# An attention and two expert layers in one program: the first tile's transposes of x moved into the drain of attention

## The chip, the cores and the metric

The program runs on one core of a Trainium2 chip. The metric is device time in microseconds of that core, from one launch to its end. Three runs of the kernel before gave 890.12, 890.15 and 888.39 us; their median is 890.12 us. Of one execution there is a profile.

## The reference, cut to what matters

Three layers follow each other: an attention with a window of 128 keys and 4 sink keys (batch 4, 8 heads, 768 positions, 64 per head), a first layer of 8 experts in which each token goes to its best expert, and a second one in which tokens are given to experts by rank up to a capacity of 384.

```
x = attention(q, k, v)                        # [3072, 512] after the heads are joined
logits = x @ w_gate + modality_bias[modality_id]
e_idx  = argmax(logits, axis=1)
gate_w = softmax(logits)[e_idx]
for e in range(8):                            # first layer of experts
    h = relu(x[e_idx == e] @ w1[e])           # 512 -> 1024
    out[e_idx == e] = gate_w * (h @ w2[e])    # 1024 -> 512
logits2 = out @ w_gate2                       # second layer: capacity 384 for each expert
out2[assigned == e] = relu(out[...] @ w21[e]) @ w22[e]
```

## The kernel before, in words

The program is written as one order of instructions for all engines; each engine takes its own in that order and waits on semaphores.

**Attention** goes over 48 groups (`NG`): a group is two blocks of 128 queries of a pair of heads. An iteration k of the loop at the end of `attention` works on several groups at once. It does the scores of group k, the transposes of the probabilities of group k-1 (`trans`, `tcopy`), the sink transposes of group k-3 (`sinktr` on TensorE, `sinkout` on ScalarE, which writes `skT`), the products with v of group k-2 (`pv`, which fills the PSUM tile `po`), and for group k-4 the copy of `po` to `oT` (ScalarE, L403), the product that makes rows of x of it (`rows`: L411 from `skT`, then L413 from `oT`, both into the PSUM tile `px`) and the division by the softmax sums (`xout`, VectorE, `rv`, `xb`, `lp`). `px` has one buffer, so `rows` of a group waits for `lp` of the group before. After the last group four more iterations run without scores: the **drain**.

**The gate** of a batch (`after_batch`) is cut into pieces `v1` to `v4` and six scatters, which a list of work in the background (`BG`) hands out: `bg.pop` takes the next piece at fixed places of the main loop. A piece that stands with a number in front waits until a model of TensorE's time has gone on by so much since the last piece. The piece `v3b` has two matmuls with the one-hot `oh` (L590, L591).

**The first expert layer** (`moe1`, which calls `Ffn.run`) goes over six tiles of 512 tokens, which are gathered from x by expert. Each tile has 8 steps; a step s does 12 matmuls of the first product into `ph` (L940) and 12 of the second into `y0` to `y3` (L883). Both operands are split into a part of full precision for the matmul and a residue: `xh`, `xl` of the tokens, `w1h`, `w1l` and `w2h`, `w2l` of the weights, `hh`, `hl` of the hidden layer. ScalarE writes the first of each, VectorE the second as the difference. `xprep` turns one of the four 128-column parts of the gathered tokens `xg` with four transposes on TensorE (L750), copies to `xh` (L751) and takes the residue `xl` (L752). The tiles 0 and 1 take tokens of the first two batches alone, so that their gathers can be issued during attention.

Before step 0, `Ffn.run` prepares the first tile: the weights of chunk 0, the four parts of x, then eight matmuls that write nothing of use (`warm`, L759), then chunk 1:

```
if i == ahead:
    src.idle()
    poll_w(1)
    for d in range(4):
        prep(js[0], d, ("tr", "ph", "y1", "y2")[d])
    if pre:
        self.warm(WARM1)
```

All tiles of this layer lie in memory that attention's tiles had, so their first writers wait for attention's last readers.

Of the kernel before, what the change touches and what calls it, by code (L numbers as in the profile page):

```python
# [21 lines left out]
NP = H // 2  # L22
# [160 lines left out]

def attention(ctx, tc, g, qT, kT, v4, vsT, vsR, wg, put_x, after_batch, bg, drain=True):
    nc = tc.nc
# [46 lines left out]
    nc.sync.dma_start(wgp, wgv)  # L232
    vst = wk.tile([128, B * NP, 96], F32, name="vst", bufs=1)
    nc.sync.dma_start(vst, vsT)
    vsx = wk.tile([96, B * NP, 72], F32, name="vsx", bufs=1)
    nc.sync.dma_start(vsx[:, :, 0:64], vsR)
# [206 lines left out]
    for k in range(NG + LRO):  # L443
# [47 lines left out]
class Gate:  # L491
# [60 lines left out]
    def after_batch(self, b, lp):  # L552
# [16 lines left out]
        def v1b():  # L569
            nc.vector.tensor_reduce(mx, lg, axis=AX.X, op=OP.max)  # L570
            nc.vector.tensor_tensor(dl, lg, bc(mx[:, :, None], [128, NB, E]), op=OP.subtract)

        def v2():
            nc.scalar.activation(ex, dl, AF.Exp)
# [159 lines left out]
class Ffn:  # L734
    def __init__(self, ctx, tc, g, tag, tpe=384, rawpool=None, vsplit=False):
        self.tc, self.nc, self.g = tc, tc.nc, g
        self.wk = ctx.enter_context(tc.tile_pool(name=tag, bufs=2))
        self.ps = ctx.enter_context(tc.tile_pool(name=tag + "p", bufs=1, space=PSUM))
        self.trbufs, self.tpe, self.vsplit = 1, tpe, vsplit
        self.rawpool = rawpool or self.wk  # L740
        self.xt = {}

    def xprep(self, j, A, xg, d, tag="tr"):
        nc, w = self.nc, 128 * A
        if d == 0:
            self.xt[j] = (self.wk.tile([128, 4, self.tpe], F32R, name="xh"), self.wk.tile([128, 4, self.tpe], F32R, name="xl"))
# [14 lines left out]
    def run(self, js, w1, w2, src, yout, hook=None, xp=((6, 0), (6, 2), (7, 0), (7, 2)), LEAD=3, LAG=2, pre=None, onx=None, more=(), mark=lambda s, n: None):  # L761
# [77 lines left out]
        def split1(c, part):  # L839
# [5 lines left out]
            if part == 0:  # L845
                ch[0][c] = (wk.tile([128, 512], F32R, name="w1h", bufs=LEAD + 2),
                            wk.tile([128, 512], F32R, name="w1l", bufs=LEAD + 2))
            h, lo = [t if small(c) else t.rearrange("p (d f) -> p d f", d=4) for t in ch[0][c]]
# [325 lines left out]
class Direct:  # L1174
# [6 lines left out]
    def load(self, i, c):  # L1181

        f, e = self.f, self.src.ereg(self.j)
        for m in (2 * c, 2 * c + 1):
            t = f.wk.tile([128, 512], F32R, name=("w1", "w2")[i] + "hl"[m % 2], bufs=4).bitcast(F32)
# [76 lines left out]

def moe1(tc, g, G, src, rt, w1, w2, wg2, wg2T):
    nc = tc.nc
    with ExitStack() as ctx:
# [52 lines left out]
        def mark(s, n):  # L1318
# [3 lines left out]
            for i in {(6, 1): (0,), (8, 1): (1,)}.get((f5, n), ()):  # L1322
# [3 lines left out]
        hook = lambda: bg.pop(2 if len(bg.q) > 12 or bg.q and isinstance(bg.q[0], tuple) else 1)  # L1326
        raw, xgs = f.run(big, w1, w2, src, yout, hook=hook, pre=(src.raw, dict(src.xg)), onx=onx, LEAD=2,
                         more=[t.j for t in small], mark=mark)
# [722 lines left out]
def tile_kernel(ctx, tc, qT, kT, v4, vsT, vsR, mid, wg, mbias, w1, w2, wg2, wg2T, w21, w22, cst, out):  # L2051
# [9 lines left out]
    with ExitStack() as c1:  # L2061
# [53 lines left out]
```

## Time and profile before

| | before |
|---|---|
| median of three runs | 890.12 us |
| runs | 888.39 to 890.15 us |
| the profiled execution's own time | 890.04 us |
| its span, first to last instruction | 888.3 us |
| TensorE busy | 841.3 us, 95% of the span |
| VectorE, ScalarE, GpSimd busy | 608.2, 386.8, 356.3 us |
| last attention matmul starts | 206.78 us |
| first matmul of the expert layer starts | 211.41 us |

A busy TensorE is not at its peak: its matmul ends are modelled, and the granted clock (PEclk on the page) tells at which of its two speeds it ran. An idle engine costs something only where another waits for it, so the table's shares say little of a change at one place; for that the timeline of the stretch from 200 to 225 us is read.

### The profile page before, as it was taken

The page shows a single profiled execution, that of the slowest core. Times are in us where ns is not written, and L with a number is a line of the kernel's source. Part 1 is how long each engine was busy: PE and PEld are TensorE (multiplying, and loading weights), DVE is VectorE, ACT ScalarE, POOL GpSimd, SP SyncE. Part 2 cuts the span into 40 slices and gives each one's busy share as a digit, 9 for nine tenths or more (in the row PEclk, how much of TensorE's full clock was granted, in tenths as well). Part 3 has the DMA queues.
Part 4 walks back from the last instruction along what each step waited for, and adds up shares of the span by engine and source line. Part 5 has one row for each costly group of instructions (what it writes and reads, how often), then busy time and mean ns, then how long its engine had stood idle before and what let it go on. Part 6 is the DMA issues. An engine that isn't in the chain of part 4 may idle for free.

```text
span 888.3 us, 15299 instructions
## 1 busy us (share of the span) xinstructions
PE 841.3 (95%) x5051; PEld 666.4 (75%) x5051; DVE 608.2 (68%) x1769; ACT 386.8 (44%) x1093; POOL 356.3 (40%) x555
## 2 busy tenths in 40 slices
PE   8889898898999999999999987999999999999997
PEld 4556666566888888888888645778788878789996
DVE  3868787876759697978886458768777776663320
ACT  3677676774334343434342214233333333445431
POOL 2776655574430202010000006535464737376561
PEclk9999999999999999999999989999999999999999
DMA  8344473549364444444346324323444424346301
GB/s 250 106 142 145 111 178 93 153 120 339 96 138 148 143 142 143 142 143 142 106 144 220 127 77 158 123 103 131 143 146 159 164 95 152 117 155 207 101 37 39
DMA packets 69774, 123.90 MB, mean 139 GB/s; under 512 B 9652, under 2 KB 22454, under 8 KB 69559
## 3 DMA queue, kind: packets, MB, share of 16 engines
q1 hardware_dynamic: 62998, 103.41, 37.1%
q0 software_dynamic: 6688, 19.43, 6.9%
q8 instruction: 42, 0.69, 0.4%
q14 instruction: 46, 0.37, 0.2%
HBM read 103.11 MB, written 19.71 MB: 138 GB/s over the span
## 4 chain that ended last, share of the span: by engine, by line
PE 74%; DVE 10%; issue 5%; ACT 4%; POOL 3%; DMA 3%; SPq 0%; POOLq 0%; DVEq 0%; ACTq 0%
PE ph L940 27%; PE y L883 26%; PE sp L306 4%; PE po L378 2%; ACT P L335 2%; PE tr L750 2%; PE rt L1569 2%; PE pt L343 2%; DMA xg<-xs,idx 1%; PE rc L1428 1%; PE px L413 1%; DVE mx L325 1%; DVE sc L150 1%; DMA vst<-in_vsT_dram 1%; DVE cmp L150 1%
## 5 line engine op out<-in xcount | busy, mean ns | idle before, releaser
L950 ACT ACTIVATE hh<-ph 128x384 fp32r<-128x384 f32 (+1 forms) x112 | 60.1, 537 | 273.7 <-PE ph L940 265.1
L940 PE MATMUL ph<-xh,w1h 128*128 128x384 f32 (+1 forms) x448 | 170.0, 380 | 0.0
L940 PE MATMUL ph<-xh,w1l 128*128 128x384 f32 (+1 forms) x448 | 162.6, 363 | 0.0
L940 PE MATMUL ph<-xl,w1h 128*128 128x384 f32 (+1 forms) x448 | 161.9, 364 | 0.0
L883 PE MATMUL y<-w2h,hh 128*128 128x512 f32 x384 | 155.5, 405 | 0.0
L883 PE MATMUL y<-w2h,hl 128*128 128x512 f32 x384 | 151.3, 394 | 0.0
L883 PE MATMUL y<-w2l,hh 128*128 128x512 f32 x384 | 151.2, 394 | 0.0
L951 DVE SCALAR_TENSOR_TENSOR hl<-ph,hh 128x384 fp32r<-128x384 f32 (+1 forms) x112 | 68.5, 611 | 107.9 <-ACT hh L950 102.1
L836 POOL TENSOR_TENSOR w2l<-w2r,w2h 128x512 fp32r<-128x512 f32 x64 | 88.7, 1393 | 64.8 <-ACT w2h L832 33.9
L1106 POOL DMA_INDIRECT xg<-xd,ent x26 | 29.1, 1120 | 189.5 <-DMA ent<-idtab 100.5
L1130 DVE SCALAR_TENSOR_TENSOR junk<-yr,wgb 128x512 f32<-128x512 f32 x160 | 103.1, 685 | 0.0
L940 PEld LDWEIGHTS ph<-xh,w1h 128*128 128x128 f32 x448 | 86.0, 192 | 10.2
L335 ACT ACTIVATE P<-sp,mx 128x132 f32<-128x132 f32 x192 | 69.0, 367 | 55.6 <-DVE mx L325 30.0
L940 PEld LDWEIGHTS ph<-xh,w1l 128*128 128x128 f32 x448 | 85.7, 191 | 9.6
L940 PEld LDWEIGHTS ph<-xl,w1h 128*128 128x128 f32 x448 | 85.0, 190 | 7.8
L883 PEld LDWEIGHTS y<-w2h,hl 128*128 128x128 f32 x384 | 72.5, 189 | 16.0
L883 PEld LDWEIGHTS y<-w2h,hh 128*128 128x128 f32 x384 | 73.1, 190 | 11.4
L883 PEld LDWEIGHTS y<-w2l,hh 128*128 128x128 f32 x384 | 72.9, 190 | 11.4
L306 PE MATMUL sp<-kr,qs 64*128 64x260 f32 (+1 forms) x384 | 60.0, 411 | 17.1 <-ACT P L335 17.0
L850 ACT ACTIVATE w1h<-w1r 128x512 fp32r<-128x512 f32 x112 | 69.7, 624 | 5.7 <-DMA w1r<-in_w_dram 3.3
L832 ACT ACTIVATE w2h<-w2r 128x512 fp32r<-128x512 f32 x112 | 69.6, 624 | 0.4 <-DMA w2r<-in_w_dram 0.4
L855 DVE TENSOR_TENSOR w1l<-w1r,w1h 128x512 fp32r<-128x512 f32 x80 | 65.5, 819 | 3.5 <-ACT w1h L850 3.5
(362 smaller groups left out, 1414.5 us busy)
## 6 DMA issues: line engine op xcount, KB each, us to landing
w1r<-in_w_dram SPq DMA_DIRECT2D x30, 1024.0 KB, 6.5
w2r<-in_w_dram SPq DMA_DIRECT2D x30, 1024.0 KB, 7.4
kr<-in_kT_dram SPq DMA_DIRECT2D x16, 396.0 KB, 3.7
qr<-in_qT_dram SPq DMA_DIRECT2D x16, 384.0 KB
vr<-in_v_dram SPq DMA_DIRECT2D x16, 384.0 KB, 4.9
xd<-xb SPq DMA_DIRECT2D x16, 384.0 KB
xs<-yr SPq DMA_DIRECT2D x24, 256.0 KB, 5.9
wgb<-in_wg2T_dram SPq DMA_DIRECT2D x1, 2048.0 KB
```

Of the source, the lines that this page charges most:

```text
L306: nc.tensor.matmul(sp[:, hd, c0:260], qs[o:o + 64, 128 * i:128 * i + 128], kr[o:o + 64, k0:k0 + 260 - c0], start=True, stop=True)
L335: nc.scalar.activation(z.P[:, n % 2, hd, :], s.sp[:, hd, 128:260], AF.Exp, bias=s.mx[:, hd:hd + 1], accum_out=z.sm[:, n % 2, hd:hd + 1])
L832: nc.scalar.activation(ch[1][c][0], r[:, q, :], AF.Copy)
L836: eng.tensor_tensor(lo, r[:, q, :], h.bitcast(F32), op=OP.subtract)
L850: nc.scalar.activation(h, v, AF.Copy)
L855: eng.tensor_tensor(lo, v, h.bitcast(F32), op=OP.subtract)
L883: nc.tensor.matmul(o, l, r, start=(first and i == 0), stop=(end and i == 2))
L940: nc.tensor.matmul(ph, wp[:, c, :], xp_[:, c, 0:NTK], start=(d == 0 and i == 0), stop=(d == 3 and i == len(cut[d]) - 1))
L950: nc.scalar.activation(hh, ph, AF.Relu)
L951: nc.vector.scalar_tensor_tensor(hl, ph, 0.0, hh.bitcast(F32), op0=OP.max, op1=OP.subtract)
L1106: self.nc.gpsimd.indirect_dma_start(out=self.xg[j][:, a, :], out_offset=None, in_=self.G.xd[0:k, :], in_offset=bass.IndirectOffsetOnAxis(a ...
L1130: nc.vector.scalar_tensor_tensor(junk, yr[:, 0:DM], 1.0, wgb[:, e, :], op0=OP.mult, op1=OP.mult, accum_out=lg[:, e:e + 1])
```

## The change

Three things are done. First, a class `Ahead` holds tiles in memory of their own: `xh0` and `xl0` for the tokens of every second tile, and two pairs of weight tiles. At the end of each of the four drain iterations, `Ahead.step` does one of the four parts of the first tile's preparation: four transposes into a PSUM tile of attention's `sp`, the copy to `xh`, the residue `xl`. In the last two of them it also splits a chunk of the first weights. Second, `Ffn.run` takes these as done: no preparation and no warm-up matmuls stand before step 0. Third, the gate pieces of the last batch each carry the number 1.4 (`SP`), so that they are spaced by the model of TensorE's time; its four empty pieces are dropped, and the exponential of that batch is a piece of its own.

```diff
+        if not live:
+            fa.step(k - NG, lambda: ps.tile([128, 2, 512], F32, name="sp", bufs=2)[:, 0])
         bg.pop(1)
-    if drain:
-        bg.drain()
...
+    def step(self, n, bank):
+        nc, src = self.nc, self.src
+        if n == 0:
+            self.x = self.xpair()
+        xh, xl = self.x
+        p, xg = bank(), src.xg[0]
+        for a in range(TPE // 128):
+            nc.tensor.transpose(p[:, 128 * a:128 * a + 128], xg[:, a, 128 * n:128 * n + 128], self.g.ident)
+        nc.scalar.activation(xh[:, n, :], p, AF.Copy)
+        nc.vector.tensor_tensor(xl[:, n, :], p, xh[:, n, :].bitcast(F32), op=OP.subtract)
+        if n in (2, 3):
+            c = n - 2
+            r = src.raw[0][0][:, :, 128 * c:128 * c + 128]
+            h, lo = self.w1[c] = self.tile("w1h", c), self.tile("w1l", c)
+            v = [t.rearrange("p (d f) -> p d f", d=4) for t in (h, lo)]
+            nc.scalar.activation(v[0], r, AF.Copy)
+            nc.vector.tensor_tensor(v[1], r, v[0].bitcast(F32), op=OP.subtract)
...
-        v = [v1, v1b, v2, v2b, v3] + [nop] * (4 if b == B - 1 else 1) + [v3b, v3c, v4]
+        v = [v1, v1b, lambda: (vx(), v2()), v2b, v3, nop, v3b, v3c, v4]
...
-            self.bg.add(*v, *[lambda f=f, h=h: (f(), h()) for f, h in zip(la, sc6)], lambda: self.done.add("x"))
+            last = [v1, v1b, vx, v2, v2b, v3, v3b, v3c, v4] + [lambda f=f, h=h: (f(), h()) for f, h in zip(la, sc6)]
+            self.bg.add(*[(SP, f) for f in last], lambda: self.done.add("x"))
...
-        ahead = 1 if pre else AHEAD
+        if pre:
+            steps = []
+            poll_w(1)
+            self.fa, self.xt[js[0]], done[0] = pre[2], pre[2].x, 2
+            for c in range(2):
+                ch[0][c] = pre[2].w1[c]
+                for n in ("w1h", "w1l"):
+                    self.ring[n] = c
...
-                if pre:
-                    self.warm(WARM1)
```

The first tiles of attention that hold the sink keys (`vst`, `vsx`) now lie in the same memory as `xh0` and `xl0`; they are read only in the first iterations.

On ScalarE the drain's instructions stood like this before (`skT` and `oT` are attention's, the `xh` rows and `w1h` belong to the expert layer):

```order
L348 ACTIVATE t_3112<-pt_3107 128x512
L397 ACTIVATE skT_3114<-sp_3105 96x128
L403 ACTIVATE oT_3157<-po_3091 128x256
L397 ACTIVATE skT_3161<-sp_3159 96x128
L403 ACTIVATE oT_3184<-po_3142 128x256
L397 ACTIVATE skT_3188<-sp_3186 96x128
L403 ACTIVATE oT_3202<-po_3169 128x256
L850 ACTIVATE w1h_3250<-w1r_3128 128x512
L751 ACTIVATE xh_3254<-tr_3256 128x512
```

After the last `oT` came the expert layer's own work. In the changed kernel the same stretch of ScalarE's queue reads:

```order
L348 ACTIVATE t_3115<-pt_3110 128x512
L397 ACTIVATE skT_3117<-sp_3108 96x128
L510 ACTIVATE xh0_3160<-sp_3162 128x512
L403 ACTIVATE oT_3169<-po_3094 128x256
L397 ACTIVATE skT_3173<-sp_3171 96x128
L510 ACTIVATE xh0_3160<-sp_3194 128x512
L403 ACTIVATE oT_3203<-po_3145 128x256
L397 ACTIVATE skT_3207<-sp_3205 96x128
L510 ACTIVATE xh0_3160<-sp_3218 128x512
L517 ACTIVATE w1h0_3225<-w1r_3131 128x512
L403 ACTIVATE oT_3232<-po_3181 128x256
L510 ACTIVATE xh0_3160<-sp_3261 128x512
```

Each of the last three `oT` now has a copy to `xh` ahead of it, the last one a `w1h` too. On TensorE the same drain, from the second of its iterations to the expert layer, stood like this before (`xg` is the first tile's gathered tokens, `px` the rows of x):

```order
L392 MATMUL sp_3159<-cst_62,psk2_174 96x128
L411 MATMUL px_3163<-bd_169,skT_3114 128x288
L413 MATMUL px_3163<-rw_165,oT_3157 128x144 x2
L378 MATMUL po_3142<-lu_3094,vr_2755 64x128 x2
...
L413 MATMUL px_3190<-rw_165,oT_3184 128x144 x2
L411 MATMUL px_3205<-bd_169,skT_3188 128x288
L413 MATMUL px_3205<-rw_165,oT_3202 128x144 x2
L750 MATMUL tr_3256<-cst_62,xg_2793 128x128 x4
```

Behind these rows came the other twelve transposes, the eight warm-up matmuls and step 0. In the changed kernel TensorE has:

```order
L509 MATMUL sp_3162<-cst_62,xg_2796 128x128 x4
L392 MATMUL sp_3171<-cst_62,psk2_177 96x128
L411 MATMUL px_3175<-bd_172,skT_3117 128x288
L413 MATMUL px_3175<-rw_168,oT_3169 128x144 x2
...
L509 MATMUL sp_3218<-cst_62,xg_2796 128x128 x4
L411 MATMUL px_3235<-bd_172,skT_3207 128x288
L413 MATMUL px_3235<-rw_168,oT_3232 128x144 x2
L509 MATMUL sp_3261<-cst_62,xg_2796 128x128 x4
L993 MATMUL ph_3291<-xh0_3160,w1h0_3225 128x512
```

Four transposes stand ahead of each remaining `rows`, the last four behind the last one, and step 0 (L993, the old L940) follows at once. Its first matmul waits for the residue `xl0` of the last part, since that is read from a bank that `ph` takes over. The two matmuls of the last batch's gate piece `v3b` move on TensorE from step 4, between its two products, to behind the first transposes of the next tile in step 6; those of the batch before stay where they were, behind the 12 matmuls of step 1.

## Rows read from the trace of the kernel before

**Rows 1.** The page's busy time of TensorE: us, share, instructions.

```profile
PE 841.3 (95%) x5051; PEld 666.4 (75%) x5051; DVE 608.2 (68%) x1769; ACT 386.8 (44%) x1093; POOL 356.3 (40%) x555
```

**Rows 2.** Timeline of TensorE, drain to step 1: start, us, line, idle and releaser.

```profile
202.82 0.31 PE L392 MATMUL sp<-cst,psk 128*96 128x128 f32 x1
...
203.10 0.65 PE L413 MATMUL px<-rw,oT 128*128 128x144 f32 x4
203.69 1.31 PE L378 MATMUL po<-lu,vr 128*64 128x128 f32 x16
204.93 0.32 PE L392 MATMUL sp<-cst,psk 128*96 128x128 f32 x1
...
206.57 0.37 PE L411 MATMUL px<-bd,skT 96*128 96x288 f32 x1 [0.71 <-DVE rv L425]
206.78 0.66 PE L413 MATMUL px<-rw,oT 128*128 128x144 f32 x4
208.09 0.63 PE L750 MATMUL tr<-cst,xg 128*128 128x128 f32 x4 [0.66 <-PE px L413]
...
209.87 1.89 PE L759 MATMUL y<-wz 128*128 128x512 bf16 x8
211.41 0.58 PE L940 MATMUL ph<-xh,w1h 128*128 128x512 f32 x1
...
214.36 0.39 PE L940 MATMUL ph<-xh,w1h 128*128 128x512 f32 x1
```

**Rows 3.** Timeline of ScalarE, drain and step 0.

```profile
202.34 0.38 ACT L403 ACTIVATE oT<-po 128x256 f32<-128x256 f32 x1 [0.32 <-PE po L378]
...
208.23 0.63 ACT L850 ACTIVATE w1h<-w1r 128x512 fp32r<-128x512 f32 x1 [2.35 <-DVE lp L431]
...
214.56 0.60 ACT L950 ACTIVATE hh<-ph 128x512 fp32r<-128x512 f32 x1 [2.71 <-PE ph L940]
```

**Rows 4.** Timeline of all engines, a part of x prepared for the second tile.

```profile
248.14 0.60 ACT L751 ACTIVATE xh<-tr 128x512 fp32r<-128x512 f32 x1
248.63 0.62 ACT L832 ACTIVATE w2h<-w2r 128x512 fp32r<-128x512 f32 x1
...
251.41 0.60 PE L750 MATMUL tr<-cst,xg 128*128 128x128 f32 x4
...
252.04 0.60 ACT L751 ACTIVATE xh<-tr 128x512 fp32r<-128x512 f32 x1 [2.78 <-PE tr L750]
...
252.67 0.69 DVE L752 TENSOR_TENSOR xl<-tr,xh 128x512 fp32r<-128x512 f32 x1 [1.13 <-ACT xh L751]
```

**Rows 5.** Timeline of TensorE, gate matmuls between steps 1 and 2, second product.

```profile
219.95 0.18 PE L590 MATMUL rt<-oh,tri 128*128 128x48 bf16 x1 [2.71 <-DVE oh L581]
...
224.41 0.39 PE L883 MATMUL y<-w2h,hh 128*128 128x512 f32 x1
```

**Rows 6.** Windows of TensorE: stretch, its us, PE busy, granted clock, DMA, GB/s.

```profile
142.00:145.40 3.40, 1.63 (x13) 1.00 0.58 220
145.40:148.80 3.40, 3.40 (x20) 0.50 0.11 31
...
208.00:212.00 4.00, 3.90 (x26) 1.00 1.02 352
...
217.20:220.00 2.80, 0.09 (x4) 1.00 0.73 276
220.50:223.90 3.40, 3.40 (x9) 0.50 0.00 0
```

**Rows 7.** Timeline of GpSimd: the first tile's last gather.

```profile
195.29 1.08 POOL L1106 DMA_INDIRECT xg<-xd,ent  x1 [0.44 <-issue]
```

**Rows 8.** Chain in order of time: the longest gather on it.

```profile
623.00 5.13 DMA xg<-xs,idx
```

**Rows 9.** Timeline of SyncE's queue: a weight load for the third tile.

```profile
267.44 0.38 SPq L730 DMA_DIRECT2D w1r<-in_w_dram  x1
```

**Rows 10.** Timeline of TensorE: the third tile's first transposes.

```profile
290.44 0.60 PE L750 MATMUL tr<-cst,xg 128*128 128x128 f32 x4
```

More of the change, by code (lines that the diff above doesn't have):

```diff
@@ L181, with attention @@
 LST, LPV, LRO = 3, 2, 4
-def attention(ctx, tc, g, qT, kT, v4, vsT, vsR, wg, put_x, after_batch, bg, drain=True):
+def attention(ctx, tc, g, qT, kT, v4, vsT, vsR, wg, put_x, after_batch, bg, fa):
     nc = tc.nc
@@ L232, in attention @@
     nc.sync.dma_start(wgp, wgv)
-    vst = wk.tile([128, B * NP, 96], F32, name="vst", bufs=1)
+    vst = fa.spare("xh", 128)[:, 0:96 * B * NP].rearrange("p (b c) -> p b c", c=96)
     nc.sync.dma_start(vst, vsT)
-    vsx = wk.tile([96, B * NP, 72], F32, name="vsx", bufs=1)
+    vsx = fa.spare("xl", 96)[:, 0:72 * B * NP].rearrange("p (b c) -> p b c", c=72)
     nc.sync.dma_start(vsx[:, :, 0:64], vsR)
@@ L479, in attention, with __init__, tile, spare @@
         at(xout, k - LRO)
+        if not live:
+            fa.step(k - NG, lambda: ps.tile([128, 2, 512], F32, name="sp", bufs=2)[:, 0])
         bg.pop(1)
-    if drain:
-        bg.drain()
+class Ahead:
+    def __init__(self, nc, g, src, pool):
+        self.nc, self.g, self.src, self.p = nc, g, src, pool
+        self.w1 = {}
+    def tile(self, name, i):
+        w = 4 * TPE if name in ("xh", "xl") else 512
+        return self.p.tile([128, w], F32R, name=f"{name}{i}", bufs=1)
+    def spare(self, name, rows):
+        return self.tile(name, 0)[0:rows].bitcast(F32)
+    def xpair(self):
+        return tuple(self.tile(n, 0).rearrange("p (d t) -> p d t", d=4) for n in ("xh", "xl"))
+    def step(self, n, bank):
[15 more added lines that the diff above has]
+            nc.vector.tensor_tensor(v[1], r, v[0].bitcast(F32), op=OP.subtract)
 TPS = 64
@@ L571, in v1b, with vx @@
             nc.vector.tensor_tensor(dl, lg, bc(mx[:, :, None], [128, NB, E]), op=OP.subtract)
+        def vx():
+            nc.scalar.activation(ex, dl, AF.Exp)
         def v2():
-            nc.scalar.activation(ex, dl, AF.Exp)
             nc.vector.tensor_scalar(dl, dl, 0.0, None, op0=OP.is_equal)
@@ L738, in __init__, with wtile @@
         self.ps = ctx.enter_context(tc.tile_pool(name=tag + "p", bufs=1, space=PSUM))
-        self.trbufs, self.tpe, self.vsplit = 1, tpe, vsplit
+        self.trbufs, self.tpe, self.vsplit, self.fa, self.ring = 1, tpe, vsplit, None, {}
         self.rawpool = rawpool or self.wk
         self.xt = {}
+    def wtile(self, name, bufs):
+        n = self.ring[name] = self.ring.get(name, -1) + 1
+        if self.fa and name in ("w1h", "w1l") and n % 4 < 2:
+            return self.fa.tile(name, n % 4)
+        return self.wk.tile([128, 512], F32R, name=name, bufs=2 if self.fa and name in ("w1h", "w1l") else bufs)
     def xprep(self, j, A, xg, d, tag="tr"):
         nc, w = self.nc, 128 * A
-        if d == 0:
+        if d == 0 and self.fa:
+            self.xt[j] = self.fa.xpair() if j % 2 == 0 else tuple(
+                self.wk.tile([128, 4, self.tpe], F32R, name=n, bufs=1) for n in ("xh", "xl"))
+        elif d == 0:
             self.xt[j] = (self.wk.tile([128, 4, self.tpe], F32R, name="xh"), self.wk.tile([128, 4, self.tpe], F32R, name="xl"))
@@ L845, in split1 @@
             if part == 0:
-                ch[0][c] = (wk.tile([128, 512], F32R, name="w1h", bufs=LEAD + 2),
-                            wk.tile([128, 512], F32R, name="w1l", bufs=LEAD + 2))
+                ch[0][c] = (self.wtile("w1h", LEAD + 2), self.wtile("w1l", LEAD + 2))
             h, lo = [t if small(c) else t.rearrange("p (d f) -> p d f", d=4) for t in ch[0][c]]
@@ L890, in run @@
         steps = [(s, part) for part in (2, 0) for s in range(-LEAD, 0)]
-        ahead = 1 if pre else AHEAD
+        if pre:
[6 more added lines that the diff above has]
+                    self.ring[n] = c
         for i, (s, part) in enumerate(steps):
-            if i == ahead:
+            if i == AHEAD:
                 src.idle()
@@ L1184, in load @@
         for m in (2 * c, 2 * c + 1):
-            t = f.wk.tile([128, 512], F32R, name=("w1", "w2")[i] + "hl"[m % 2], bufs=4).bitcast(F32)
+            t = f.wtile(("w1", "w2")[i] + "hl"[m % 2], 4).bitcast(F32)
             r = slice(128 * (m % 4), 128 * (m % 4) + 128)
@@ L1260, in keep, with moe1 @@
         self.rt.keep(self.i, self.rt.LG[:, NMAIN + self.i])
-def moe1(tc, g, G, src, rt, w1, w2, wg2, wg2T):
+def moe1(tc, g, G, src, rt, w1, w2, wg2, wg2T, fa):
     nc = tc.nc
@@ L1326, in moe1 @@
         hook = lambda: bg.pop(2 if len(bg.q) > 12 or bg.q and isinstance(bg.q[0], tuple) else 1)
-        raw, xgs = f.run(big, w1, w2, src, yout, hook=hook, pre=(src.raw, dict(src.xg)), onx=onx, LEAD=2,
+        raw, xgs = f.run(big, w1, w2, src, yout, hook=hook, pre=(src.raw, dict(src.xg), fa), onx=onx, LEAD=2,
                          more=[t.j for t in small], mark=mark)
@@ L1372 @@
 JC, NIT, FEW, IDLE = 64, 4, 2, 4
-WARM, WARM1 = 14, 8
+WARM = 14
 SLACK = 0.5
@@ L1378 @@
 X0 = 2.0
-SC = 6
+SC, SP = 6, 1.4
 CM = 0.2, 0.7, 1.3
@@ L2066, in tile_kernel @@
         bg.add(*late_consts(nc, g), *rt.setup())
+        fa = Ahead(nc, g, src, c1.enter_context(tc.tile_pool(name="ahead", bufs=1)))
         with ExitStack() as c2:
-            attention(c2, tc, g, qT, kT, v4, vsT, vsR, wg, G.put_x, G.after_batch, bg, drain=False)
-        moe1(tc, g, G, src, rt, w1, w2, wg2, wg2T)
+            attention(c2, tc, g, qT, kT, v4, vsT, vsR, wg, G.put_x, G.after_batch, bg, fa)
+        moe1(tc, g, G, src, rt, w1, w2, wg2, wg2T, fa)
     bad = moe2(tc, g, rt, w21, w22, out)
```

## The prediction

> **What bounds the kernel now.** I read the page's table of engines first: TensorE is busy for 95% of the span [rows 1], so the time is TensorE's own work plus the few places where it waits, and a change is worth what it takes from or adds to TensorE's line of time. Then the timeline of TensorE over the change's place. The drain's four products that make rows of x (L413) start at 203.10, a second and third between, and 206.78; the transposes of x start at 208.09 after a wait of 0.66 us, the warm-ups at 209.87, step 0 at 211.41 [rows 2]. So from the last L413 to step 0 it takes 4.63 us, and this is what the change attacks. Next, the wait behind it: after step 1 TensorE stands 2.71 us for the one-hot of the third batch's gate (L581) and then needs 4.46 us, 219.95 to 224.41, for 12 matmuls [rows 5] that took 2.95 us as step 0's, 211.41 to 214.36 [rows 2]. The windows say why: TensorE was busy 0.09 of 2.80 us, and in 220.5 to 223.9 the granted clock was 0.50, which is 1.2 instead of 2.4 GHz [rows 6]. From 224.41 on TensorE is busy without a wait of note until the second expert layer; so whatever moves the start of step 0 moves the end by as much, unless the gate's wait swallows it.
>
> It does not swallow it. The chain to that one-hot hangs on the end of step 0: ScalarE takes `hh` at 214.56 [rows 3], and the gate's matmuls start 5.39 us later [rows 5]; the built order has the same VectorE rows between the two as before. Step 0 later by d is the gate later by d.
>
> **The change part by part.**
>
> *What goes.* The wait of 0.66 us, 1.78 us of transposes (208.09 to 209.87) and 1.54 us of warm-ups (209.87 to 211.41) leave the path behind the last L413 [rows 2].
>
> *What comes into the drain.* Four transposes precede each remaining L413, but these are not the price. On ScalarE each of the last three `oT` now stands behind a copy to `xh`, and that copy waits for the last of the four transposes, which stand on TensorE behind all of the iteration's products with v. L413 waits for `oT`. So each iteration becomes one chain in series: transposes, `xh`, `oT`, L413. Its lengths come from a part of x prepared in the steady state: `xh` starts 0.63 us after the transposes (251.41 to 252.04), the next ScalarE instruction 0.49 us after `xh` (248.14 to 248.63), `xl` 0.63 us after `xh` and it lasts 0.69 us [rows 4]; an `oT` lasts 0.38 us [rows 3]. For the hop from `oT` to the matmul that loads it I put 0.1 us, an estimate: TensorE restarted 0.10 us after VectorE's last piece ahead of the transposes. Together 1.60 us from the transposes to L413.
>
> Now the four slots. (1) The transposes stand where the sink transpose stood, 202.82; L413 starts at 204.42 instead of 203.10 [rows 2], 1.32 us late. (2) From L413 through the products with v it took 1.83 us (203.10 to 204.93) [rows 2]; the next transposes start at 206.25, their L413 at 207.85. (3) L413 itself takes 0.59 us (203.10 to 203.69) [rows 2]; transposes at 208.44. Here a `w1h` stands between `xh` and `oT`; I give it the pitch of a copy, 0.49 us, since it is of the same size (0.63 against 0.60 us [rows 3, 4]). L413 starts at 208.44 + 1.60 + 0.49 = 210.53; before it was 206.78 [rows 2]. (4) Transposes at 211.12, `xh` at 211.75, `xl` from 212.38 to 213.07. The first matmul of step 0 waits for that `xl`; with 0.1 us it starts at 213.2. That is 1.8 us after 211.41 [rows 2]. The sum is a loss of 3.75 us at the last L413 against a gain of 2.0 us behind it (2.64 us from L413 to step 0, not 4.63).
>
> Ends of this: it would be 1.3 us if each hop were 0.1 us shorter than I put it (five of them), 2.4 us if each slot took 0.15 us longer.
>
> *What the chain needs from DMAs.* The first tile's last gather was issued by 196.37 [rows 7]; the longest gather wait that the trace's chain shows is 5.13 us [rows 8], which makes 201.5, ahead of 202.82. The weights: `w1h` ran at 208.23 [rows 3] and in the change it runs at about 209.6. Nothing there.
>
> *VectorE in the drain* gets four `xl` and a `w1l` of about 0.7 us. `px` needs the `lp` of the slot before; with slots of 3 us in place of 2 there is room, so I put nothing.
>
> *No warm-ups.* Before, TensorE was busy 3.90 of the 4 us from 208 to 212 and kept clock 1.00 [rows 6]. In the change, from 209.2 to 213.2 it has the end of a slot, one L413 and four transposes, 1.5 us of work by the sum above. Two rows bound what follows: in attention it was busy 1.63 of 3.40 us and the next 3.4 us went at 0.50; behind 0.09 of 2.80 us likewise [rows 6]. Step 0 can lose nothing, or at most what the slow 12 matmuls lost, 4.46 - 2.78 = 1.7 us (2.78 being 0.06 for the gate's two and 12 at the 0.23 us pitch of step 0) [rows 2, 5]. The 1.5 us in 4 is nearer to the row with the fall than to the one without, so I take a fall, and half its price, 0.85 us: the slow stretch may begin before step 0 or end in step 1, and what it takes from step 1 the gate's wait covers.
>
> A row and a rule stand side by side here. The row with 16 transposes and eight warm-ups shows full clock, and cannot separate the two [rows 6]. The Trainium skill, page "TensorE: Matmul & The Clock Gate", section "Part 4: PE-mode transpose", says that transposes do not count as TensorE activity in the way matmuls do. By that rule the stretch ahead of step 0 is emptier than its busy time says, all of step 0 goes slow, and the sum would be 1.8 + 1.7 instead of 1.8 + 0.85 us.
>
> *The last batch's pieces, spaced.* TensorE does not wait in steps 3 to 7, so there is nothing to gain there, and the gate's two matmuls cost it as much at the new place. The third tile's ids are now asked for behind the weight load of 267.44 [rows 9]; with about 4 us for the ids and a wait for gathers of 5.13 us [rows 8] plus four issues of 1.1 us [rows 7] they are there by 281, and the tile's transposes come at 290.44 [rows 10]. 9 us of cover, cost nothing. If the pieces were late by more than that, TensorE would wait for the remainder.
>
> *Other memory for the tiles* changes no count of buffers: nothing.
>
> Sum against the profiled execution: 890.04 + 1.8 + 0.85 = 892.7 us. That execution is 0.08 us below the median of the runs shown, 890.12, so I leave it.
>
> **The rivals.**
>
> A, the clock holds: slots as worked out, no fall. 890.04 + 1.8 = 891.8 us. For it: the clock stayed at 1.00 through the drain before, with its waits of 0.71 and 0.66 us [rows 2]. Against it: the drain's waits are now longer.
>
> B, all of step 0 at half clock, 890.04 + 1.8 + 1.7 = 893.5 us. The sentence cited above would make it so.
>
> C, the drain absorbs the work and the kernel is faster. Place: `oT` on ScalarE. If `xh` ended before `oT` had its input, the last L413 would stay near 206.78; with the row's 0.59 and the chain of step (4) of 2.05 us, step 0 starts at 209.4 and the time is 888.0 us. It decides from the point where the transposes of a slot are over before the products with v of the same slot are. For it: TensorE idles 0.71 us in the drain [rows 2]. Against: `oT` found its input at 202.34 [rows 3], and `xh` can't start before 203.45.
>
> D, half of C: slots shorter than worked out, step 0 later by 0 to 1 us, 890.6 us.
>
> E, a late gate: gathers of the third tile over their cover, or more slow stretches; 895 us.
>
> **How the numbers follow.** The forecast has a chance of 0.38, A 0.26, B 0.13, C 0.07, D 0.12, E 0.04. What a measurement of this kernel can tell from no change is about 0.2%, 1.8 us: 888.3 to 891.9. C lies on the lower bound, most of it below: faster 0.06. D is within, A lies on the upper bound and more than half of it within: 0.31. The rest is slower: 0.63. For a range that leaves out 2 in 10, C and E go, and the edges of B and D: 890.2 to 894.2 us.
>
> **What would show it.** Right: in the profile after, L413 of the last three slots starts at about 204.4, 207.9 and 210.5 and ends an idle stretch that `oT` released; each `oT` starts right behind an `xh`; step 0 starts near 213.2, released by VectorE's `xl`; the granted clock falls between 212 and 217, and again after the gate's wait, which is still about 2.7 us. Wrong: step 0 before 211.4 (C), `oT` ahead of its `xh` in time, a wait of TensorE at the third tile's transposes (E), or a gate wait that has shrunk, which would mean that its chain does not hang on step 0.

## The result, and the profile after

The changed kernel is slower: 895.25 us, median of 7 runs (892.2 to 901.4), against 889.38 us of the kernel before (885.46 to 891.36, 7 runs): ratio 1.0075, 95% interval 1.0049 to 1.0100. The forecast was 892.7 us, with a range up to 894.2; the time lies above the range. The direction was right, the size was not: +5.9 us where +2.7 stood. Two runs in the series below, of 4402.21 and 946.77 us, were far slower than all others and count in no ratio.

The profiled execution took 898.11 us (before: 890.04) with a span of 896.3 us. TensorE's busy time, for [rows 1]:

```profile
PE 844.7 (94%) x5043; PEld 667.6 (74%) x5043; DVE 611.8 (68%) x1769; ACT 386.5 (43%) x1093; POOL 354.2 (40%) x555
```

It is 3.4 us longer with eight matmuls fewer. Step 0 at half clock, which the prediction had foreseen, is 1.45 us of that; so matmuls have become slower elsewhere too, which it had not.

The timeline of TensorE in the changed kernel, drain to step 0, answers to [rows 2] (start, us, line, tiles, idle before and who ended it):

```profile
199.81 0.33 PE L343 MATMUL pt<-cst,P 128*128 128x128 f32 x1
...
203.41 0.76 PE L413 MATMUL px<-rw,oT 128*128 128x144 f32 x4 [0.72 <-ACT oT L403]
204.09 1.31 PE L378 MATMUL po<-lu,vr 128*64 128x128 f32 x16
205.33 0.66 PE L509 MATMUL sp<-cst,xg 128*128 128x128 f32 x4
...
206.95 0.76 PE L413 MATMUL px<-rw,oT 128*128 128x144 f32 x4 [0.72 <-ACT oT L403]
207.54 0.60 PE L509 MATMUL sp<-cst,xg 128*128 128x128 f32 x4
...
209.62 0.76 PE L413 MATMUL px<-rw,oT 128*128 128x144 f32 x4 [0.84 <-ACT oT L403]
210.22 0.60 PE L509 MATMUL sp<-cst,xg 128*128 128x128 f32 x4
212.23 0.80 PE L993 MATMUL ph<-xh,w1h 128*128 128x512 f32 x1 [1.41 <-DVE xl L511]
...
216.63 0.39 PE L993 MATMUL ph<-xh,w1h 128*128 128x512 f32 x1
```

ScalarE beside it, for [rows 3]:

```profile
206.03 0.60 ACT L510 ACTIVATE xh<-sp 128x512 fp32r<-128x512 f32 x1 [2.51 <-PE sp L509]
206.52 0.38 ACT L403 ACTIVATE oT<-po 128x256 f32<-128x256 f32 x1
...
208.68 0.62 ACT L517 ACTIVATE w1h<-w1r 128x512 fp32r<-128x512 f32 x1
209.19 0.38 ACT L403 ACTIVATE oT<-po 128x256 f32<-128x256 f32 x1
```

Each of these `oT` starts right behind an `xh`, the last one behind the `w1h` that follows it, and each L413 waits for `oT`. In this execution attention ended 1.03 us earlier than in the profile before (its last transposes of P, L343, at 199.81 for 200.84). With that added, the three L413 stand at 204.44, 207.98 and 210.65 and step 0 at 213.26; the prediction had 204.42, 207.85, 210.53 and 213.2.

The windows of the changed kernel for [rows 6] (stretch, its us, busy us of PE, PEld, DVE, ACT and POOL, granted clock, DMA, GB/s), and the gate for [rows 5]:

```profile
205.30:208.70 3.40, 2.41 (x17) 1.83 (x15) 1.47 (x5) 1.55 (x5) 2.48 (x4) 1.00 1.02 342
208.70:212.10 3.40, 1.28 (x9) 0.96 (x8) 2.69 (x8) 2.12 (x6) 0.66 (x2) 1.00 1.06 397
212.10:215.50 3.40, 3.27 (x8) 2.60 (x9) 0.68 (x2) 0.39 (x1) 0.00 (x0) 0.51 1.03 327
...
222.30:225.70 3.40, 3.40 (x10) 2.72 (x10) 3.07 (x15) 0.81 (x2) 0.00 (x0) 0.51 0.00 0
```

```profile
222.27 0.18 PE L628 MATMUL rt<-oh,tri 128*128 128x48 bf16 x1 [2.76 <-DVE oh L619]
```

Behind 1.28 us of work in 3.40 the clock falls to half (1.2 GHz) just as step 0 begins; its 12 matmuls take 4.40 us (212.23 to 216.63), not 2.95. The first eight of them are slow. The gate's wait is as long as before.

So far the mechanism is the forecast one, with a larger price for step 0. The rest shows only when the shift between the two kernels is followed along the program. The table is worked out from start times in the profiles, in us: P is attention's last transpose of P (L343), step 0 its first matmul, h the `hh` on ScalarE of steps 0, 2 and 47 (the last of the first layer with full tiles), gate its first matmul, last the last `hh` of the second layer. It starts at P because attention's own end differs between executions, from 197.24 to 201.06 us in these profiles.

| profile of | P to step 0 | step 0 to h0 | h0 to gate | gate to h2 | h2 to h47 | P to h47 | h47 to last |
|---|---|---|---|---|---|---|---|
| before | 10.57 | 3.15 | 5.39 | 4.66 | 255.25 | 279.02 | 395.80 |
| changed | 12.42 | 4.60 | 5.44 | 4.74 | 257.92 | 285.12 | 398.67 |
| changed, again | 12.42 | 4.63 | 5.45 | 4.72 | 257.81 | 285.03 | 398.04 |
| pad | 12.42 | 4.44 | 5.44 | 4.63 | 255.87 | 282.81 | 399.24 |
| before, pad 128 | 10.57 | 3.18 | 5.43 | 4.67 | 259.43 | 283.28 | 396.27 |
| before, pad 64 | 10.57 | 3.14 | 5.43 | 4.43 | 256.10 | 279.67 | 395.21 |
| zeros ahead of step 0 | 12.51 | 3.04 | 5.45 | 3.17 | 257.90 | 282.08 | 397.70 |
| oT first | 10.46 | 5.53 | 5.48 | 3.16 | 257.93 | 282.55 | 398.69 |
| before, spaced | 10.56 | 3.17 | 5.39 | 4.67 | 255.96 | 279.74 | 394.77 |
| changed, unspaced | 12.42 | 4.63 | 5.45 | 4.72 | 257.53 | 284.74 | 398.46 |
| three costs away | 9.94 | 3.04 | 5.44 | 4.70 | 255.83 | 278.95 | 397.25 |
| same, gate filled | 9.94 | 3.04 | 5.45 | 3.15 | 255.92 | 277.50 | 399.16 |
| same kernel again | 9.95 | 3.05 | 5.45 | 3.15 | 256.19 | 277.78 | 395.21 |
| before, gate filled | 10.57 | 3.15 | 5.39 | 3.10 | 255.50 | 277.72 | 397.62 |

Against before, the changed kernel loses 1.85 us in the drain, 1.45 in step 0, 0.13 around the gate and 2.67 over the first layer: 6.10 us. Then 2.87 more in the second layer and 0.04 behind it, less 1.03 of attention, is the 7.98 us between the two spans.

The 2.67 us come without a wait of TensorE over 0.3 us. The timeline of two neighbouring steps of the changed kernel, each with its first and last matmul of the first product (12 of them, 11 pitches):

```profile
264.61 0.40 PE L993 MATMUL ph<-xh,w1h 128*128 128x512 f32 x1
264.85 0.40 PE L993 MATMUL ph<-xh,w1l 128*128 128x512 f32 x1
...
267.17 0.40 PE L993 MATMUL ph<-xl,w1h 128*128 128x512 f32 x1
267.40 0.40 PE L931 MATMUL y<-w2h,hh 128*128 128x512 f32 x1
...
269.02 0.39 PE L931 MATMUL y<-w2l,hh 128*128 128x512 f32 x1
...
270.15 0.39 PE L993 MATMUL ph<-xh,w1h 128*128 128x512 f32 x1
270.38 0.39 PE L993 MATMUL ph<-xh,w1l 128*128 128x512 f32 x1
...
272.65 0.39 PE L993 MATMUL ph<-xl,w1h 128*128 128x512 f32 x1
```

2.56 / 11 is 233 ns, 2.50 / 11 is 227 ns. The slow steps are the 24 of 48 in which x lies in one pool and w1 in the other, here x in the layer's own pool and w1 in the prepared one. The built program gives the places: the prepared pool's tiles begin at 128 modulo 256 bytes within a partition (110208 for `xh`, 126592 for `w1h`), the layer's own at 0 modulo 256 (192256 and 184064). In the kernel before, all are at 0.

The second product between the two steps (L931) has both of its operands at 0 modulo 256, and yet its first seven matmuls go at (269.02 - 267.40) / 7 = 231 ns, and only the last five at 1.13 / 5 = 226. Behind the slow steps of the other mix (x prepared, w1 not) the first three are slow. So the start of what follows a slow first product is slow too.

### The profile page after: what moved, and what is told of

It is laid out like the page before. It is cut to its first block, busy times and chain, and to the rows that moved or that the text cites. A ratio compares the mean times of both kernels' runs of the same rounds, so it can differ in the third digit from the quotient of the medians.

```text
span 896.3 us, 15279 instructions
## 1 busy us (share of the span) xinstructions
PE 844.7 (94%) x5043; PEld 667.6 (74%) x5043; DVE 611.8 (68%) x1769; ACT 386.5 (43%) x1093; POOL 354.2 (40%) x555
## 4 chain that ended last, share of the span: by engine, by line
PE 70%; DVE 14%; issue 5%; ACT 5%; POOL 3%; DMA 2%; SPq 0%; POOLq 0%; DVEq 0%; ACTq 0%
PE ph L993 26%; PE y L931 25%; PE sp L306 3%; ACT P L335 2%; PE po L378 2%; PE tr L799 2%; PE rt L1622 2%; DMA xg<-xs,idx 1%; PE rc L1481 1%; DVE sc L150 1%; DVE mx L325 1%; PE pt L343 1%; DVE junk L1183 1%; PE px L413 1%; DVE cmp L150 1%
## 5 line engine op out<-in xcount | busy, mean ns | idle before, releaser
L993 PE MATMUL ph<-xh,w1h 128*128 128x384 f32 (+1 forms) x448 | 171.9, 384 | 1.4 <-DVE xl L511 1.4
L993 PE MATMUL ph<-xh,w1l 128*128 128x384 f32 (+1 forms) x448 | 164.4, 367 | 0.0
L993 PE MATMUL ph<-xl,w1h 128*128 128x384 f32 (+1 forms) x448 | 162.7, 365 | 0.0
L931 PE MATMUL y<-w2h,hh 128*128 128x512 f32 x384 | 155.7, 405 | 0.0
L931 PE MATMUL y<-w2h,hl 128*128 128x512 f32 x384 | 151.9, 396 | 0.0
L931 PE MATMUL y<-w2l,hh 128*128 128x512 f32 x384 | 151.7, 395 | 0.0
L993 PEld LDWEIGHTS ph<-xh,w1h 128*128 128x128 f32 x448 | 86.7, 194 | 12.1 <-DVE xl L511 1.6
L993 PEld LDWEIGHTS ph<-xh,w1l 128*128 128x128 f32 x448 | 86.6, 193 | 10.2
L993 PEld LDWEIGHTS ph<-xl,w1h 128*128 128x128 f32 x448 | 85.5, 191 | 8.4
L931 PEld LDWEIGHTS y<-w2h,hl 128*128 128x128 f32 x384 | 72.8, 190 | 16.3
L931 PEld LDWEIGHTS y<-w2h,hh 128*128 128x128 f32 x384 | 73.0, 190 | 11.7
L931 PEld LDWEIGHTS y<-w2l,hh 128*128 128x128 f32 x384 | 72.9, 190 | 11.8
```

Source lines behind the costliest of these rows:

```text
L931: nc.tensor.matmul(o, l, r, start=(first and i == 0), stop=(end and i == 2))
L993: nc.tensor.matmul(ph, wp[:, c, :], xp_[:, c, 0:NTK], start=(d == 0 and i == 0), stop=(d == 3 and i == len(cut[d]) - 1))
```

## The experiments

Ratios are to the kernel before, run beside them, with 95% intervals.

**Pad in the changed kernel.** One line ahead of the first layer's own tiles, so that all operands are at 128 modulo 256:

```
         bg = G.bg
+        f.wk.tile([128, 32], F32, name="pad", bufs=1)
         wgb = gate_rows(nc, f, wg2T)
```

> The changed kernel, with one unused tile of 128 bytes per partition ahead of the tiles of the first expert layer's own pool; nothing else differs. Theory M (relative placement of a matmul's two operands): in the changed kernel the matmuls of the first product (ph) go at a pitch of 233 ns in the 24 of 48 steps whose operands lie in different pools, and at 227 ns in the others; in those 24 the addresses of x and w1 within a partition differ by 128 modulo 256, in the others by 0. With the pad all of them lie at 128 modulo 256: 227 ns in every step, and the shift from the kernel before no longer grows from 224 to 470 us (it grew by 2.6 us). Time 895.2 - 2.6 = 892.6 us. Rival R (it is the other pool itself, its distance or its region, whatever the alignment): pitch unchanged, 895.2 us. Rival N (the drift is not in the matmuls but in what else runs beside them): pitch unchanged or other steps slow, 895.2 us.

Ratio 1.0022 (0.9995 to 1.0048). The step that stood in the pools' mix goes at 2.49 / 11 = 226 ns, as in the kernel before:

```profile
261.46 0.39 PE L993 MATMUL ph<-xh,w1h 128*128 128x512 f32 x1
...
263.95 0.39 PE L993 MATMUL ph<-xl,w1h 128*128 128x512 f32 x1
```

So do all steps but those that hold the next tile's transposes, which go at 228 to 231 ns here as in the kernel before. The pools are as far apart as they were. h2 to h47 falls by 2.05 us, to 0.62 above before, and not by 2.67. Theory M holds; 0.6 us have another cause. The times can't tell 2.05 from 2.67: the interval of the ratio alone is 4.7 us wide.

**The same pad in the kernel before, between w1 and x.**

```
+            if self.vsplit and j == 0 and self.tpe == TPE:
+                self.wk.tile([128, 32], F32, name="pad", bufs=1)
             self.xt[j] = (self.wk.tile(...
```

> The kernel before, with one unused tile of 128 bytes per partition between the tiles of w1 and those of x in the first expert layer's pool; nothing else differs. Theory M: x then lies at 128 modulo 256 and w1h and w1l at 0, in all 48 steps: pitch 233 ns instead of 227 in every first product, 48 x 12 x 6 ns = 3.4 us, so 889.4 + 3.4 = 892.8 us; the second product, whose two operands move together, stays. Rivals R and N: the kernel before stays as it is, 889.4 us and 227 ns.

Ratio 1.0042 (1.0016 to 1.0068): 3.7 us for 3.4 expected, with nothing else changed. Every step is now slow (2.56 / 11 = 233 ns):

```profile
264.72 0.40 PE L942 MATMUL ph<-xh,w1h 128*128 128x512 f32 x1
...
267.28 0.40 PE L942 MATMUL ph<-xl,w1h 128*128 128x512 f32 x1
```

h2 to h47 is 4.18 us longer; what is above 3.4 lies in the second product, which did not stay as expected: its operands moved together, but its first matmuls behind each slow first product are slow here too. Rivals R and N fall.

**64 bytes in place of 128**, the same line with 16 for 32:

> The kernel before with a pad of 64 bytes per partition in place of 128: x at 64 modulo 256, w1 at 0. The pitch of the first product tells how the cost depends on the difference. M1 (any difference modulo 256 costs the same): 232 ns as with 128. M2 (only a difference that is not a multiple of 64 or of 32 costs less or nothing): 227 ns. M3 (graded): about 229 to 230 ns.

One run, 886.65 us. The pitch is 2.53 / 11 = 230 ns, half way to 233: M3, graded. h2 to h47 grows by 0.85 us, a fifth of the 4.18; the second product stays at 227 ns here, except beside the transposes.

```profile
263.65 0.39 PE L942 MATMUL ph<-xh,w1h 128*128 128x512 f32 x1
...
266.18 0.39 PE L942 MATMUL ph<-xl,w1h 128*128 128x512 f32 x1
```

**Six matmuls on zeros ahead of step 0**, on a bank of attention's, behind its loop:

```
         bg.pop(1)
+    warm(6)
```

> The changed kernel, with six matmuls on zeros behind attention's last transposes, in the wait of 1.41 us for the last xl that stands ahead of step 0 (six at the 0.19 us of the former ones are 1.2 us). Theory K (the empty stretch ahead of step 0 costs the clock): granted clock 1.00 in step 0, which takes 2.95 us instead of 4.40; its start stays within 0.3 us; time 895.2 - 1.45 = 893.8 us, and the gate's one-hot comes as much earlier. Rival L (the six alone are too little after the waits of the three slots before): the clock falls all the same, 895.2 us. Rival G (the gain comes back at the gate's wait, whose chain hangs on something else): step 0 is faster, the wait of 2.76 us grows to 4.2, 895.2 us.

Ratio 1.0056 (1.0032 to 1.0079). The windows show the clock at its full level (2.4 GHz) through step 0, and also behind the gate's wait:

```profile
208.70:212.00 3.30, 2.49 (x14) 1.51 (x14) 2.70 (x8) 2.02 (x5) 0.41 (x2) 1.00 1.04 394
212.00:215.00 3.00, 2.92 (x13) 2.44 (x14) 0.53 (x1) 0.24 (x1) 0.00 (x0) 1.00 1.13 348
...
220.50:223.50 3.00, 2.93 (x14) 2.44 (x14) 2.73 (x13) 0.91 (x2) 0.00 (x0) 1.00 0.00 0
```

Step 0 to h0 is 3.04 us for 4.60, and it starts 0.09 later. Theory K holds, L and G fall. The lack of warm-ups had cost 1.5 us.

P to h47 falls by 3.04 us, twice what was expected. The other half is behind the gate's wait, 3.17 us for 4.74, though TensorE waits there for 2.8 us as before. With oT first (next) the clock holds there too. So the fall behind this wait, which the prediction took as given, came in nine of the eleven profiles in which nothing fills the wait.

**oT first.** The transposes stay; the copies of a part go behind the next slot's `oT` and `skT`, `xl` and `w1l` behind its rows:

```
         at(sinkout, k - LST)
+        if k > NG:
+            fa.copy(k - NG - 1)
...
         at(xout, k - LRO)
+        if k > NG:
+            fa.rest(k - NG - 1)
```

> The changed kernel, with the copies of each prepared part put behind the next slot's oT and skT on ScalarE, and xl and w1l behind the next slot's rows on VectorE; the transposes stay where they are, and w1h goes with the second and third part. Theory S (the price of the drain is that oT stands behind xh): the three L413 no longer wait for a copy, slots of about 2 us as in the kernel before; step 0 is then bound by VectorE behind the last L413 (rows of x 0.6, xl, w1l, xl of 0.69 each: about 3.4 us behind it), 1.2 us earlier than in the kernel before and 3.05 us earlier than in the changed one: 895.2 - 3.05 = 892.2 us, and 890.7 us if the clock then holds through step 0. Rival T (the slots are as long because of the transposes' bank, which waits for the xl of the part before, or of the products with v): L413 again 3 us apart, 895.2 us. Rival V (the copies delay the next slot's skT or the sums instead): a gain of at most 1 us, 894.2 us.

Ratio 1.0056 (1.0031 to 1.0080): less than expected.

```profile
200.80 0.66 PE L413 MATMUL px<-rw,oT 128*128 128x144 f32 x4
...
203.36 0.65 PE L413 MATMUL px<-rw,oT 128*128 128x144 f32 x4
...
205.08 0.76 PE L413 MATMUL px<-rw,oT 128*128 128x144 f32 x4
205.68 0.60 PE L514 MATMUL sp<-cst,xg 128*128 128x128 f32 x4
208.54 0.80 PE L1006 MATMUL ph<-xh,w1h 128*128 128x512 f32 x1 [2.26 <-DVE xl L528]
...
213.83 0.63 PE L1006 MATMUL ph<-xh,w1h 128*128 128x512 f32 x1
```

No L413 waits now, and step 0 comes 1.96 us earlier than in the changed kernel: S is right on what the price was. But the slots are TensorE's own work, transposes and products with v, so the last L413 came 2.8 us earlier than in the changed kernel and still 1.1 later than in the one before (counted from P); then step 0 waits 2.26 us for VectorE, and behind that wait all of it runs at half clock (208.54 to 213.83, 5.29 us). The expectation had the length behind the last L413 right (3.4 us, 3.46 measured) and had taken the slots ahead of it as no longer than before.

**Only the spacing, in the kernel before** (the exponential is a piece of its own and the empty pieces are gone, as in the change).

```
-        v = [v1, v1b, v2, v2b, v3] + [nop] * (4 if b == B - 1 else 1) + [v3b, v3c, v4]
+        v = [v1, v1b, lambda: (vx(), v2()), v2b, v3, nop, v3b, v3c, v4]
...
+            self.bg.add(*[(SP, f) for f in last], lambda: self.done.add("x"))
```

> The kernel before, with one part of the change alone: the last batch's gate pieces spaced by 1.4 us of TensorE time. Theory P (nothing waits there, as predicted): ratio 1.000, no new wait of TensorE between 224 and 470 us. Rival Q (the changed kernel with the pad still drifted by 0.6 us between 270 and 327 us; that is the pieces' work): the same drift here, ratio 1.0007, which the times cannot tell, so the drift in the trace is what decides.

Ratio 1.0028 (1.0001 to 1.0056). TensorE has a wait that the kernel before has not, the third tile's second transposes:

```profile
293.85 0.33 PE L753 MATMUL tr<-cst,xg 128*128 128x128 f32 x1 [0.48 <-DVE xl L755]
```

The windows say who is late: the kernel before, then this one. In the kernel before, VectorE had 0.16 us free in 282 to 297. With the pieces spaced it does 1.81 us less in the stretch ahead, and later has nothing free.

```profile
267.00:282.00 15.00, 15.00 (x68) 12.43 (x67) 13.93 (x40) 6.04 (x12) 0.00 (x0) 1.00 0.46 135
282.00:297.00 15.00, 15.00 (x72) 12.33 (x72) 14.84 (x38) 5.24 (x10) 0.00 (x0) 1.00 0.43 148
```

```profile
267.00:282.00 15.00, 15.00 (x68) 12.43 (x67) 12.12 (x37) 6.04 (x12) 4.55 (x4) 1.00 0.53 164
282.00:297.00 15.00, 14.52 (x68) 11.71 (x68) 15.00 (x41) 5.53 (x11) 0.00 (x0) 1.00 0.51 160
```

h2 to h47 grows by 0.71 us: Q. The ratio stands for 2.5 us, of which the trace shows no more than these 0.7; the interval reaches down to 0.1.

**Only the spacing undone, in the changed kernel** (the two lines above, turned round):

> The changed kernel with one part undone: the last batch's gate pieces stand as in the kernel before, not spaced. Theory Q (the spacing costs 0.7 us: VectorE, which has no gap from 282 to 297 us, gets to the third tile's xl later): the wait of 0.48 us for xl at the third tile's transposes is gone, the growth of the shift from 224 to 470 us is 1.95 us instead of 2.66; ratio 1.0072 if the changed kernel's is 1.0080. Rival W (the spacing pays elsewhere, and costs nothing in sum): the growth stays at 2.6 us, ratio 1.0080.

Ratio 1.0064 (1.0032 to 1.0096). The wait that the changed kernel has there is gone:

```profile
296.46 0.66 PE L799 MATMUL tr<-cst,xg 128*128 128x128 f32 x4 [0.27 <-DVE xl L801]
```

h2 to h47 shrinks by 0.3 to 0.4 us, not 0.7. The times can't tell so little.

**The changed kernel once more.**

> The changed kernel itself once more, unchanged, for more runs of it beside the kernel before. Sum so far: drain chain 1.85 us, half clock in step 0 1.45 us, pitch of the first product 2.6 us, together 5.9 us: ratio 1.0066. Rival (a fourth cost in the second expert layer, where the profiled execution of the changed kernel had a slow stretch and a wait that the kernel before had not, 3.7 us): if it belongs to the change the ratio is 1.010, and if it is chance the second layer's shift differs in this profile.

895.52 us, ratio 1.0084 (1.0055 to 1.0114). Everything up to h47 repeats within 0.1 us; the second layer does not (398.67, then 398.04), nor do the places of its half-clock stretches (741.2 us, then 730.9).

**All three costs taken away**: pad, oT first with the transposes on two banks in turn and the second `w1l` behind the last `xl`, six matmuls on zeros.

```
+            fa.step(k - NG, lambda: ps.tile([128, 512], F32, name="pt") if (k - NG) % 2 else
+                    ps.tile([128, 2, 512], F32, name="sp", bufs=2)[:, 0])
...
-        if n in (1, 2):
+        if n in (1, 3):
```

> The changed kernel with its three costs taken away together: the pad of 128 bytes; oT and skT ahead of the copies on ScalarE, rows of x ahead of xl on VectorE, the second w1l behind the last xl, and the transposes alternating between two banks; six matmuls on zeros in the wait ahead of step 0. Theory S+K+M: last L413 to step 0 takes 2.9 us instead of 3.46 as with oT first alone, so step 0 comes 0.7 us earlier than in the kernel before, counted from the last full products with v; clock 1.00 in step 0; pitch 227 ns. Ratio 0.9992. Rival U (the changed kernel costs something beside these three, in the second layer for one): ratio 1.002 to 1.003, at the same gain in the drain.

Ratio 1.0003 (0.9977 to 1.0029). P to step 0 is 0.63 us shorter than before (0.7 expected), and P to h47 the same as before less 0.07: h2 to h47 is 0.58 us longer, as in the other versions with the spacing, and takes the drain's gain. Neither theory is decided by the time; by the trace, the change without its three costs is a draw.

**That version, pieces unspaced, and the gate's wait filled with ten matmuls on zeros:**

```
+            pz = g.pst()
+            for _ in range(10 if b == B - 2 else 0):
+                nc.tensor.matmul(pz, g.wz[:, 0:128], g.wz, start=True, stop=True)
```

> The version with the three costs taken away (pad, oT first, six matmuls on zeros), with two edits more: the last batch's gate pieces stand as in the kernel before, not spaced; and ten matmuls on zeros stand ahead of the third batch's gate matmuls, in TensorE's wait of 2.76 us for the one-hot. Theory: step 0 comes 0.66 us earlier than in the kernel before; the wait of 0.48 us and the late xl of the third tile at 290 to 297 us are gone (0.7 us against the version without these edits); behind the gate's wait the clock stays at 1.00, so the 12 matmuls that took 4.46 us take 2.95, 1.5 us: together 2.1 us less than the kernel before, ratio 0.9976. Rival X (the matmuls on zeros make the gate's two late, or the clock falls somewhere else instead): ratio 0.999 to 1.000.

> The version with the three costs taken away, the pieces unspaced and the gate's wait filled, once more and unchanged, since its first interval reaches from 0.995 to 1.001. If its gain of the first layer (3.0 us earlier than the kernel before at the end of that layer, 2.5 of them from the change's place and the gate) reaches the end, the ratio is 0.997 to 0.998 again; if the second layer takes it back, 1.000 or over.

Ratios 0.9980 (0.9951 to 1.0009) and 0.9985 (0.9963 to 1.0006), medians 887.15 and 887.44 for 888.98 and 888.67. Gate to h2 is 3.15 us for 4.66, P to h47 shorter than before by 1.52 and 1.24 us (the expectation's 2.5 had counted some of attention's own earlier end). It is not 2.1, because the second tile's transposes, now earlier, wait for an `xl`, 0.48 us in the first profile and 0.77 in the second:

```profile
244.49 0.66 PE L816 MATMUL tr<-cst,xg 128*128 128x128 f32 x4 [0.48 <-DVE xl L818]
```

The two series point the same way, and each interval alone reaches past 1. The second execution has 395.21 us in the second layer, the first 399.16, of one program.

**The filling alone, in the kernel before.**

> The kernel before with one edit: ten matmuls on zeros ahead of the third batch's gate matmuls, in TensorE's wait of 2.71 us. Theory: the granted clock stays at 1.00 behind the wait and the 12 matmuls of step 2 take 2.95 us in place of 4.46: 1.5 us, ratio 0.9983. Rival X: the clock falls all the same, ratio 1.000.

The clock holds, as in the other two profiles with the wait filled, and X falls:

```profile
214.30:217.20 2.90, 2.40 (x11) 1.00 (x11) 2.38 (x11) 1.42 (x4) 0.00 (x0) 1.00 0.73 276
217.30:220.20 2.90, 2.90 (x15) 2.38 (x15) 2.64 (x12) 0.77 (x2) 0.00 (x0) 1.00 0.03 6
```

Gate to h2 is 3.10 us for 4.66, P to h47 1.30 us shorter. Yet the ratio is 1.0023 (0.9996 to 1.0050), where 0.9983 was expected: the gain of the first layer is not seen in the time. In the profiled execution the second layer took 397.62 us for 395.80, more than the gain, but one program's executions differ by more than that (395.21 and 399.16 above), so why it is not seen stays open.

## Why the prediction missed

*The drain: right, and to a tenth.* Forecast 1.8 us, measured 1.85, with the slots at their times. The prediction speaks of four L413 from 203.10 on; there are three (203.10, 205.21 and 206.78, and one ahead of them at 201.15), and its slots are worked out for three, so the sum stands. Counted from P, the last L413 came 3.9 us later than before; in the version with oT first, where no L413 waits for `oT`, it came 1.1 us later, so 2.8 of them were the place of oT behind the copies, and the rest is mostly the transposes' own time on TensorE.

*No warm-ups: right in kind, mis-sized.* I took half the price, 0.85 us; it was 1.45, and this term of the sum failed by its size. The reason for the half, that the slow stretch might begin early or end in step 1, did not come true: the granted clock is 0.51 from 212.1 to 215.5, and step 0 began at 212.23, so nearly all of it fell there. Nor was the 1.7 us that I called the most it could lose a bound: with oT first all 12 matmuls went slow, and the step took 5.29 us for 2.95. The matmuls on zeros give 1.5 us back. The row shows a fall behind 1.28 us of work in 3.40, with four transposes among its nine matmuls. By the rule cited in the prediction (the Trainium skill, "TensorE: Matmul & The Clock Gate", "Part 4: PE-mode transpose") all of step 0 goes slow. The trace agrees in the outcome for eight of the 12 matmuls, and no run here separates the transposes' part from the waits'.

*The gate's wait: right.* 2.71 to 2.76 us; h0 to gate is 5.39 to 5.48 us in all profiles. Step 0 later by d was the gate later by d, and step 0 earlier by d, the gate earlier by d. Only the fall of the clock behind it is not as sure as I took it to be (gate to h2 is 3.2 us in two versions that put nothing into this wait).

*"Other memory for the tiles changes no count of buffers: nothing": this step failed.* It cost 2.0 us (the pad takes 2.05 away; 24 steps of 12 matmuls at 6 ns are 1.7, the rest lies in the second product right behind them). I had asked how many buffers there are and not where they lie.

*"9 us of cover, cost nothing" of the spaced pieces: failed too, by 0.3 to 0.7 us.* The cover of the gathers was there; what moved was VectorE's work, in a stretch where VectorE had 0.16 us to spare. I had looked at TensorE's waits there and not at VectorE's load. The sign named for rival E, a wait at the third tile's transposes, did come, but it was 0.27 us long and for VectorE's `xl`, not for a gather. Neither of the two steps had been given a bound, so the range held nothing of them.

Sum of the forecast with the measured terms: 890.04 + 1.85 + 1.45 + 0.13 + 2.67 = 896.1 us, against 895.25 and 895.52 in two series; as a difference 6.10 us, against 5.87 and 6.85 beside the kernel before in the same series. Of the rivals none had this cause; E's 895 us is near by chance, for no gather came late and no transposes of the third tile waited for one.

*Open.* The second layer took 394.8 to 396.3 us in five of the 14 profiles and 397.3 to 399.2 in the other nine. The windows from 716 to 760 us tell the two groups apart: the granted clock there is 1.00 in all of the five and 0.92 or 0.96 in all of the nine. These are the kernel before, the changed one, and the two executions of the version with the gate filled, columns as above:

```profile
716.00:760.00 44.00, 42.30 (x269) 35.74 (x269) 32.18 (x92) 17.37 (x40) 25.16 (x22) 1.00 0.40 132
716.00:760.00 44.00, 40.23 (x251) 33.87 (x250) 32.15 (x82) 15.90 (x37) 20.82 (x21) 0.96 0.36 119
716.00:760.00 44.00, 42.32 (x261) 35.69 (x260) 30.07 (x91) 16.12 (x39) 26.45 (x22) 0.96 0.39 132
716.00:760.00 44.00, 41.55 (x265) 34.83 (x264) 32.48 (x90) 16.73 (x38) 25.36 (x22) 1.00 0.40 132
```

So the longer second layer goes with one or two more falls of the clock. Of the nine profiles with the prepared tile eight have such a fall, of the five of the kernel before and its variants one, that with the gate filled. The instructions of the second layer are the same in both kernels, and so are the places of all their operands but one small one (`wgc`). One program is on both sides, so part is chance. Whether the change makes such a fall more likely, the runs don't settle.

## What to carry to other kernels

When a change moves tiles to another pool, compare the addresses of the two operands of the matmuls that read them, modulo 256: here 128 bytes of padding were worth 2 to 4 us of 890. A thing that fills a wait (the warm-ups) is priced by what the clock does behind it; here, with the stretch ahead emptied, half the price was too little. And where work is only re-spaced, look at the load of the engine that does it in the place where it lands, not only at the waits of the engine that sets the time.

## What the runs showed of the hardware

In the first product the pitch of an fp32r matmul of 128 by 512 depended on the relative place of its stationary and its moving operand within a partition: 227 ns with no difference modulo 256 bytes, 229 to 230 with 64 (one run), 233 with 128; other differences were not tried. Absolute place and distance did not matter there: with both at 128 it was 227, across two pools as within one. But a matmul's own two operands are not all that counts: behind a slow first product the first seven matmuls of the second went at 231 ns with operands that lie alike.

The Trainium skill, "TensorE: Matmul & The Clock Gate", "Step-by-step: what each phase is for", says that the weight load and the moving operand have read ports of their own, so that loading the next weights takes no read bandwidth from the running matmul. These rows speak against a full independence of the two reads, if it is these two that meet; no run here shows which reads do.
